# Folding every local product on GpSimd ahead of VectorE's sums, and output weights kept in dead key and query tiles

## The chip, the cores and the metric

The kernel runs on one core of a Trainium2 chip. A core has TensorE (matrix products, PE in the profile, with its weight loads as PEld), VectorE (DVE), ScalarE (ACT), GpSimd (POOL) and SyncE (SP), whose queue here issues nearly all DMAs. Each engine works through its own list of instructions in order and waits on the others through semaphores. The metric is the time of one execution on the device in microseconds, lower is better. Before the change the median of three runs is 921.38 us (920.93 to 921.93).

## The reference

Two attentions over the same x (2048 tokens, 448 columns, 16 heads of 28) are mixed by a gate of each token. Branch A looks at 8 keys per query, two tokens apart, backwards; branch B at all 2048 keys.

```python
def _A_ref(x, wqkv, wo):                       # W, dil = 8, 2
    q, k, v = qkv[0], qkv[1], qkv[2]
    idx = pos[:, None] - off[None, :]          # off = arange(W) * dil
    logits = jnp.einsum("bhsd,bhswd->bhsw", q, kg) * scale
    logits = jnp.where(mask[None, None, :, :], logits, -1e9)
    attn = _softmax(logits, axis=-1)
    o = jnp.einsum("bhsw,bhswd->bhsd", attn, vg)
    return o.transpose(0, 2, 1, 3).reshape(B, S, D) @ wo
def _B_ref(x, wqkv, wo):
    scores = jnp.einsum("bhqd,bhkd->bhqk", q, k) * (Dh ** -0.5)
    o = jnp.einsum("bhqk,bhkd->bhqd", _softmax(scores, axis=-1), v)
    return o.transpose(0, 2, 1, 3).reshape(B, S, D) @ wo
g = _sigmoid((x * gate_w).sum(-1, keepdims=True))
return g * a + (1 - g) * b
```

## The kernel before

All of it is float32 made from two halves: a value is split into a rounded part ("hi") and the rest ("lo"), and a product is three matmuls, hi·hi, hi·lo and lo·hi.

**Projection (to about 260 us).** q, k and v of both branches are formed and written to DRAM scratch (`qk_hi`, `qk_lo`, `a_scr`); v of branch B stays in the tile `V`.

**The 256 steps (about 260 to 843 us).** Branch B goes in 16 units u = 4·g + b, for head group g of four heads and query block b of 512. A unit has 16 steps, one for each block of 128 keys, so program step st = 16·u + kt. A step has, on TensorE, 12 score matmuls (four heads, three terms, L959) into pairs of PSUM banks, up to three matmuls of a first, rough pass over a later unit (L142, "maxima"), and the product of the step before with V (L925). ScalarE takes exp of two heads at a time (L962, two a step). VectorE takes the maximum of the rough scores from PSUM, one of 512 columns and one of 1024 a step (L146). The maxima of a unit are negated on GpSimd (`nmt`, L178), turned, stored and loaded back as two extra rows of the query tile `QH`, so that the exponent is already shifted. 320 of the 1024 rough tiles are done during the projection and three in each step after, so they end in step 234; the last 21 steps have scores, exp and V alone. This text calls these the bare steps. The key tiles `KH[1]`, `KH[2]`, `KL[0]` and the rough query tiles `QP[0]` have no reader in the last 40 steps.

**Branch A beside it.** Eight column groups c (two heads each) times eight offsets w. GpSimd multiplies q with the shifted k (`a_score`, L599, 128x896); for some (c, w) it also adds the upper 14 of each 28 columns onto the lower ("folds", L604, 128x448). VectorE sums along the row (`a_reduce`, L609): four pieces of 8 rows by 28 where the product is not folded, two of 16 rows by 14 where it is; each piece reads 224 elements. `NR[c, w]` holds the number of pieces: 2 for c < 2 and for odd w, else 4. Then come a softmax over w (`a_softmax`, shared by GpSimd, VectorE and ScalarE) and the weighted sum of v (`a_av`, L649 and L654, GpSimd alone), stored to `oa_scr`.

**What sets the order.** The steps are written out by hand; `at(place, st, f)` hangs a piece of work on a step ("pre" ahead of the scores, "dve" and "act" behind them, "end" last). Branch A is placed by a planner: `item` gives each piece an engine, a key (its wished step), an estimated cost and what it needs; `issue` emits pieces in the order of the keys while a running debt, `late`, stays under a limit (4.2 for GpSimd, `DLIM` for VectorE). The debt falls by `step` in each step and grows by the estimated cost, and for VectorE by a share for the rough maxima. The estimates order the work; they cost nothing themselves.

**The end.** When branch A is finished (`a_done`, program step 217 before), its memory is given back; the seven blocks of output weights `wo` are loaded (L742) and split by one ScalarE copy (L746) and one GpSimd subtraction (L747) each. After step 255 sixteen output tiles j follow (`op_tile`): the branch A rows are transposed (L781) and split, and 21 matmuls (L803) add both branches. `op_load_b(b, k)` brings piece k of branch B's normalised rows of query block b, `op_load_a(j)` those of branch A. A unit's result is finished in small pieces (`fin_*`): a copy of the V product on ScalarE (`osb`, L821), its sums through DRAM, a product and a subtraction on GpSimd (L850, L858) and a ScalarE copy (`onhi`, L854).

Of the kernel before, what the change touches and what calls it, by code (L numbers as in the profile page):

```python
# [25 lines left out]
def gated_mix_kernel(ctx: ExitStack, tc: tile.TileContext, xT, xn, gw, wA, wB, woAB, out):  # L26
# [568 lines left out]
    def a_score(c, w):  # L595
        if w == 0:
            Lt[c] = a2.tile([128, W, NJ, 2], F32, name="L", bufs=3)
        p = a3.tile([128, NJ, 56], F32, tag="prod", name="prod")
        nc.gpsimd.tensor_tensor(out=p, in0=qt[c], in1=kvt["k", c % 2][:, HALO - DIL * w:HALO - DIL * w + NJ, :],  # L599
                                op=ALU.mult)  # L600
        prods[c, w] = p.rearrange("p j (h d) -> p (j h) d", d=DH)
        if NR[c, w] == 2:
            lo, hi = prods[c, w][:, :, 0:DH // 2], prods[c, w][:, :, DH // 2:]
            nc.gpsimd.tensor_tensor(out=lo, in0=lo, in1=hi, op=ALU.add)  # L604
            prods[c, w] = lo
# [64 lines left out]
    for c in range(8):  # L670
        for w in range(W):
            NR[c, w] = 2 if w % 2 or c < 2 else 4
    last = lambda c, w: ("r", c, w, NR[c, w] - 1)
    for c in range(8):
        c0 = CH * c
# [4 lines left out]
        for w, o in enumerate((0, 2, 5, 8, 11, 14, 17, 20)):  # L680
            back = (c, w - 4) if w > 3 else (c - 1, w + 4)
            item("pool", c0 + o, ("s", c, w), 2.05 + 1.0 * (NR[c, w] == 2),
                 [(("ld", "k", c), 4), (("ld", "q", c), 4), (("a", c - 3, 7, 0), 0), (("s", c, w - 1), 0)]
                 + ([(last(*back), 0)] if back in NR else []), lambda c=c, w=w: a_score(c, w))
            for i in range(NR[c, w]):
                item("dve", c0 + o + 2 + 0.1 * i, ("r", c, w, i), 0.32,
                     [(("s", c, w), 3), (("r", c, w, i - 1) if i else last(c, w - 1) if w else ("r",), 0)],
                     lambda c=c, w=w, i=i: a_reduce(c, w, i, NR[c, w]))
# [7 lines left out]
        for w in range(W):  # L696
            for part in ((0,) if w == 0 else (0, 1)):
                item("pool", c0 + 30 + 1.4 * n, ("a", c, w, part), 1.65 if part == 0 else 2.05,
# [27 lines left out]
    A_START, DLIM, LOOK = 5, 0.7, 40  # L726
# [3 lines left out]
    wo = []  # L730
    wor = {}
    oP = {}

    def load_wo():
        actx.close()
        oP["1"] = ctx.enter_context(tc.tile_pool(name="wop", bufs=1))
        oP["2"] = ctx.enter_context(tc.tile_pool(name="wop2", bufs=2))
        wo.extend(oP["1"].tile([128, 7, D], F32R, name=f"wo{i}") for i in range(2))
# [5 lines left out]
    def split_wo(k):  # L744
        raw = wor.pop(k)[:, :D]
        nc.scalar.activation(wo[0][:, k, :], raw, AF.Copy)  # L746
        nc.gpsimd.tensor_tensor(out=wo[1][:, k, :], in0=raw, in1=wo[0][:, k, :].bitcast(F32), op=ALU.subtract)  # L747

    def a_done(st):
        adone.append(st)  # L750
        load_wo()

        d = -(st + 6) % NJ + 2 if (st + 6) % NJ > NJ - 7 else 0
        for k in range(7):
            at("pre", st + d + k + 1, lambda k=k: raw_wo(k))
            at("act", st + d + 6 + k, lambda k=k: split_wo(k))
# [41 lines left out]
    def op_mm(j, bank, ks, first=False, last=False):  # L798
        b, jj = divmod(j, 4)
        for k in ks:  # L800
            for i, (a, c) in enumerate(TERMS):
                src = oaT[j][a][:, 128 * k:128 * k + 128] if k < 3 else onT[b][k - 3][a][:, 128 * jj:128 * jj + 128]
                writes(bank, nc.tensor.matmul(bank[:, :D], src, wo[c][:, k, :],  # L803
# [92 lines left out]
    def op_tile(j, behind):  # L896
# [9 lines left out]
        if 4 <= j < 12:  # L906
            op_load_b(b + 1, j % 4)
# [58 lines left out]
    for u in range(NU):  # L966
        g, b = divmod(u, NB)
        for kt in range(NJ):
# [44 lines left out]
            step = 2.25 if left else 2.1  # L1013
            late["dve"] = max(0.0, late["dve"] + 0.58 * min(3, left) - step)
# [35 lines left out]
```

## Time and profile before

| what | before |
|---|---|
| median of 3 runs | 921.38 us |
| span of the profiled execution | 921.0 us |
| its own time, by the same start and end | 921.0 us, 0.38 us under the median |
| TensorE busy | 911.3 us (99%) |
| VectorE busy | 731.6 us (79%) |
| ScalarE busy | 649.8 us (71%) |
| GpSimd busy | 624.0 us (68%) |
| granted TensorE clock | 0.999 |

The shares are means over stages with different limits. Matmuls are pipelined, so a TensorE that is shown busy may still be late; whether a step could be shorter is read from the time between its exps, and what a step waits for from the waits. The order of instructions, shown below, tells where something stands in an engine's list, not when it runs.

### The profile page before, as it was taken

Reading aid. Unit: us, or ns where it says so; the run is one execution under the profiler, and the core shown is the slowest. Engines: PE = TensorE matmul, PEld = TensorE weight load, DVE = VectorE, ACT = ScalarE, POOL = GpSimd, SP = SyncE. Lnnn points to the kernel's source line nnn. Section 1 sums busy time; section 2 is a strip of 40 time slices with the busy share of each in tenths; the row PEclk is TensorE's granted clock in tenths of the full one; section 3 lists DMA queues with packets and bytes.
Section 4 is the critical chain, followed back from the end, with each engine's and each line's share of the span. In section 5 each row is a group of like instructions: output and inputs, shape, how many; then the busy total and the mean of one; then the engine's idle time right before and its main releaser. Section 6 shows DMA issues by size and latency. Waiting matters only on the chain.

```text
span 921.0 us, 21402 instructions
## 1 busy us (share of the span) xinstructions
PE 911.3 (99%) x8390; PEld 547.3 (59%) x8390; DVE 731.6 (79%) x975; ACT 649.8 (71%) x797; POOL 624.0 (68%) x488
## 2 busy tenths in 40 slices
PE   8999999999999999999999999999999999999998
PEld 6799999998944444444444444444444444335997
DVE  6488999998979999999999999999998888501221
ACT  6456434343378888888888888888989889996221
POOL 2389846464469799999999999999994851300100
PEclk9999999999999999999999999999999999999999
DMA  9877503559462342235135232431312123441572
GB/s 264 276 247 193 158 12 82 142 132 97 116 241 64 101 121 51 84 105 129 41 94 157 83 102 61 132 84 26 106 47 53 33 50 100 135 132 51 158 218 87
DMA packets 103966, 105.11 MB, mean 114 GB/s; under 512 B 64136, under 2 KB 73736, under 8 KB 103080
## 3 DMA queue, kind: packets, MB, share of 16 engines
q1 hardware_dynamic: 103720, 103.47, 41.5%
q8 instruction: 66, 1.08, 0.5%
q10 hardware_dynamic: 144, 0.26, 0.1%
q14 instruction: 36, 0.29, 0.1%
HBM read 62.72 MB, written 40.96 MB: 113 GB/s over the span
## 4 chain that ended last, share of the span: by engine, by line
PE 96%; DMA 2%; DVE 1%; ACT 1%; issue 0%; SPq 0%; ACTq 0%; DVEq 0%
PE T L959 31%; PE av L925 27%; PE r L295 15%; PE T L803 7%; PE r L290 6%; PE r L142 4%; PE T L142 4%; DMA V<-in_xT 1%; PE T L781 1%; DMA KH<-qk_hi 0%; DMA qk_hi<-qkh 0%; ACT P L962 0%; DVE xl L212 0%; SPq L99 0%; DVE MX L159 0%
## 5 line engine op out<-in xcount | busy, mean ns | idle before, releaser
L962 ACT ACTIVATE P<-T 128x1024 f32<-128x1024 f32 x512 | 497.0, 1024 | 66.0 <-PE T L959 64.9
L146 DVE TENSOR_REDUCE MX<-T 128x1 f32<-128x512 f32 x470 | 443.4, 954 | 39.2 <-PE T L959 16.4
L925 PE MATMUL av<-P,V 128*32 128x512 f32 x2048 | 272.7, 605 | 0.4 <-ACT osb L821 0.4
L959 PEld LDWEIGHTS T<-QH,KH 30*128 30x128 f32 x1024 | 92.5, 181 | 238.4 <-ACT P L962 197.5
L959 PE MATMUL T<-QH,KH 30*128 30x512 f32 x1024 | 222.9, 492 | 0.2 <-ACT P L962 0.2
L142 PE MATMUL T<-KH,QP 28*128 28x512 f32 x704 | 222.6, 463 | 0.1
L159 DVE TENSOR_REDUCE MX<-r 128x2 f32<-128x1024 f32 x160 | 192.1, 1222 | 27.1 <-PE r L142 23.4
L959 PE MATMUL T<-QH,KL 28*128 28x512 f32 x1024 | 190.8, 391 | 0.0
L959 PE MATMUL T<-QL,KH 28*128 28x512 f32 x1024 | 190.2, 392 | 0.0
L599 POOL TENSOR_TENSOR prod<-qt,kt 128x896 f32<-128x896 f32 x64 | 135.1, 2115 | 4.8 <-DMA kt<-a_scr 4.8
L358 ACT ACTIVATE raw<-r 128x896 f32<-128x896 f32 (+1 forms) x64 | 58.9, 921 | 99.4 <-PE r L295 93.7
L654 POOL TENSOR_TENSOR oat<-oat,prod 128x896 f32<-128x896 f32 x56 | 118.2, 2110 | 2.4
L142 PEld LDWEIGHTS T<-KH,QP 28*128 28x128 f32 x704 | 86.0, 181 | 23.2 <-ACT P L962 10.2
L359 POOL TENSOR_TENSOR ast<-raw 128x448 f32<-128x448 f32 x48 | 55.5, 1155 | 60.3 <-ACT raw L358 50.6
L649 POOL TENSOR_TENSOR prod<-vt,L 128x896 f32<-128x896 f32 x56 | 95.4, 1704 | 0.6
L959 PEld LDWEIGHTS T<-QH,KL 28*128 28x128 f32 x1024 | 93.5, 183 | 0.7
L959 PEld LDWEIGHTS T<-QL,KH 28*128 28x128 f32 x1024 | 93.4, 184 | 0.0
L925 PEld LDWEIGHTS av<-P,V 128*32 128x32 f32 x2048 | 40.3, 108 | 79.9 <-issue 66.8
L295 PE MATMUL r<-wh,xh 64*128 64x448 f32 (+1 forms) x512 | 82.8, 363 | 0.3 <-ACT raw L358 0.3
L142 PE MATMUL r<-KH,QP 64*128 64x512 f32 x320 | 80.5, 394 | 2.0 <-DMA KH<-qk_hi 0.8
L295 PE MATMUL r<-wh,xl 64*128 64x448 f32 (+1 forms) x384 | 70.4, 364 | 0.0
L295 PEld LDWEIGHTS r<-wh,xh 64*128 64x128 f32 x512 | 63.2, 185 | 1.5 <-ACT raw L358 0.6
(101 smaller groups left out, 1049.9 us busy)
## 6 DMA issues: line engine op xcount, KB each, us to landing
a_scr<-ast SPq DMA_DIRECT2D x24, 448.0 KB
qk_hi<-qkh SPq DMA_DIRECT2D x24, 256.0 KB
qk_lo<-qkh SPq DMA_DIRECT2D x24, 256.0 KB
rbc<-rs SPq DMA_DIRECT2D x64, 64.0 KB
QP<-qk_hi SPq DMA_DIRECT2D x64, 56.0 KB
KL<-qk_lo SPq DMA_DIRECT2D x16, 224.0 KB
QH<-qk_hi SPq DMA_DIRECT2D x64, 56.0 KB
QL<-qk_lo SPq DMA_DIRECT2D x64, 56.0 KB
```

Source lines behind the costliest of these rows:

```text
L142: nc.tensor.matmul(bank, qhis[u][h % 2][r, 128 * qs:128 * qs + 128], KH[u // NB % 3][r, 512 * kc:512 * kc + 512], start=True, stop=True)
L146: nc.vector.tensor_reduce(MX[:, n % NMX:n % NMX + k], bank, axis=X, op=ALU.max)
L159: nc.vector.tensor_reduce(m, PM[k], axis=X, op=ALU.max)
L295: nc.tensor.matmul(bank[:, 0:cols], x, ws[c][rows, k, 0:cols], start=first, stop=last)
L358: nc.scalar.activation(raw[:, :, 0:cols], PJ[n % 2][:, :, 0:cols], AF.Copy)
L599: nc.gpsimd.tensor_tensor(out=p, in0=qt[c], in1=kvt["k", c % 2][:, HALO - DIL * w:HALO - DIL * w + NJ, :], op=ALU.mult)
L649: nc.gpsimd.tensor_tensor(out=dst.rearrange("p j (h d) -> p j h d", d=DH), in0=kvt["v", c % 2][:, HALO - DIL * w:HALO - DIL * w + NJ, :].r ...
L654: nc.gpsimd.tensor_tensor(out=oat[c], in0=oat[c], in1=oat[c, w], op=ALU.add)
L803: writes(bank, nc.tensor.matmul(bank[:, :D], src, wo[c][:, k, :], start=(first and k == ks[0] and i == 0), stop=(last and k == ks[-1] and ...
L925: nc.tensor.matmul(av[32 * h:32 * h + 32, :], V[:, kt, 4 * g + h, :], tiles_[h], start=(kt == 0), stop=(kt == NJ - 1), skip_group_check=True)
L959: nc.tensor.matmul(bank[a], (KH[g % 3], KH[g % 3], KL[g % 2])[t][r, ks], (qh, ql, qh)[t][r, :], start=(t == 0), stop=(t == 2))
L962: nc.scalar.activation(p, one if a == "2" else mine, AF.Exp, scale=SCALE)
```

## The change

1. `NR` is 2 for all 64 products. GpSimd folds the 24 that it did not fold (c of 2 and above, even w), and VectorE sums each of these in two pieces instead of four. The planner's estimate for a product becomes 3.15, VectorE's limit `DLIM` goes from 0.7 to 0.6, its share for each rough tile from 0.58 to 0.6, and `step` from 2.25 to 2.2. The products and loads of c = 7 get keys five steps earlier.
2. The 14 pieces of the output weights have no tiles of their own. They lie in 448-column slices of `KH[1]`, `KH[2]`, `KL[0]` and the two tiles `QP[0]`. Their loads hang on steps 232 to 238 and their splits on steps 237 to 243, whenever branch A ends; before, both hung on the end of branch A, which put the splits on steps 226 to 232. The subtraction of the split moves from GpSimd to VectorE.
3. `a_done` falls on step 241. The first query block's rows (`op_load_b(0, k)`) are loaded four steps long after it, in place of steps 231 to 234; the second block's rows are loaded within output tiles 0 to 3, in place of steps 237 to 240. The first branch A rows are loaded at step 246, as before.

```diff
-        if NR[c, w] == 2:
-            lo, hi = prods[c, w][:, :, 0:DH // 2], prods[c, w][:, :, DH // 2:]
+        for n in (DH // 2, DH // 4)[:3 - NR[c, w]]:
+            lo, hi = prods[c, w][:, :, 0:n], prods[c, w][:, :, n:2 * n]
             nc.gpsimd.tensor_tensor(out=lo, in0=lo, in1=hi, op=ALU.add)
             prods[c, w] = lo
...
-            NR[c, w] = 2 if w % 2 or c < 2 else 4
+            NR[c, w] = 2
...
-        c0 = CH * c
+        c0 = CH * c - 5 * (c == 7)
...
-            item("pool", c0 + o, ("s", c, w), 2.05 + 1.0 * (NR[c, w] == 2),
+            item("pool", c0 + o, ("s", c, w), 3.15 + 0.5 * (NR[c, w] == 1),
...
-    A_START, DLIM, LOOK = 5, 0.7, 40
+    OP0 = NJ * (NU - 2)
+    WO_AT = OP0 + 8
+    A_START, DLIM, LOOK = 5, 0.6, 40
...
-    wo = []
+    spare = [t[:, D * i:D * i + D] for t in (KH[1], KH[2], KL[0]) for i in range(4)] + [t[:, :D] for t in QP[0]]
+    wo = [spare[:7], spare[7:]]
...
     def split_wo(k):
         raw = wor.pop(k)[:, :D]
-        nc.scalar.activation(wo[0][:, k, :], raw, AF.Copy)
-        nc.gpsimd.tensor_tensor(out=wo[1][:, k, :], in0=raw, in1=wo[0][:, k, :].bitcast(F32), op=ALU.subtract)
+        nc.scalar.activation(wo[0][k], raw, AF.Copy)
+        nc.vector.tensor_tensor(out=wo[1][k], in0=raw, in1=wo[0][k].bitcast(F32), op=ALU.subtract)
 
     def a_done(st):
         adone.append(st)
-        load_wo()
-
-        d = -(st + 6) % NJ + 2 if (st + 6) % NJ > NJ - 7 else 0
-        for k in range(7):
-            at("pre", st + d + k + 1, lambda k=k: raw_wo(k))
-            at("act", st + d + 6 + k, lambda k=k: split_wo(k))
+        assert st < OP0 + 24, st
+        actx.close()
+        oP["2"] = ctx.enter_context(tc.tile_pool(name="wop2", bufs=2))
+        for k in range(4):
+            at("end", st + 1 + k, lambda k=k: op_load_b(0, k))
+        at("end", st + 5, lambda: (op_load_a(0), op_load_a(1)))
+
+    for k in range(7):
+        at("pre", WO_AT + k, lambda k=k: raw_wo(k))
+        at("act", WO_AT + 5 + k, lambda k=k: split_wo(k))
...
-        if 4 <= j < 12:
+        if j < 12:
             op_load_b(b + 1, j % 4)
...
-    OP0 = NJ * (NU - 2)
-    for k in range(4):
-        at("end", OP0 + 7 + k, lambda k=k: op_load_b(0, k))
-        at("end", OP0 + 13 + k if k < 3 else OP0 + 16, lambda k=k: op_load_b(1, k))
-    at("end", OP0 + 22, lambda: (op_load_a(0), op_load_a(1)))
...
-            step = 2.25 if left else 2.1
-            late["dve"] = max(0.0, late["dve"] + 0.58 * min(3, left) - step)
+            step = 2.2 if left else 2.1
+            late["dve"] = max(0.0, late["dve"] + 0.6 * min(3, left) - step)
```

VectorE's list in the middle of the steps, before: `MX` rows are the two maxima of a step (128x1 and 128x2), `L<-prod` rows the sums of branch A; "x2" is two in a row.

```order
L609 TENSOR_REDUCE L<-prod 128x16 x2
L146 TENSOR_REDUCE MX<-T_3274 128x1
L146 TENSOR_REDUCE MX<-T_3266 128x2
L146 TENSOR_REDUCE MX<-T_3274 128x1
L146 TENSOR_REDUCE MX<-T_3262 128x2
L609 TENSOR_REDUCE L<-prod 128x8 x2
L146 TENSOR_REDUCE MX<-T_3274 128x1
L146 TENSOR_REDUCE MX<-T_3266 128x2
L609 TENSOR_REDUCE L<-prod 128x8
L146 TENSOR_REDUCE MX<-T_3274 128x1
```

The same list at about the same place, after:

```order
L609 TENSOR_REDUCE L<-prod 128x16
L146 TENSOR_REDUCE MX<-T_3274 128x1
L146 TENSOR_REDUCE MX<-T_3262 128x2
L609 TENSOR_REDUCE L<-prod 128x16
L146 TENSOR_REDUCE MX<-T_3274 128x1
L146 TENSOR_REDUCE MX<-T_3266 128x2
L609 TENSOR_REDUCE L<-prod 128x16
L146 TENSOR_REDUCE MX<-T_3274 128x1
L146 TENSOR_REDUCE MX<-T_3262 128x2
```

Where steps had none, one or two sums, each now has one at most; over the whole list 63 steps had two, and the sums reach to step 222 where they ended at step 199.

ScalarE's list, before, at the steps that held the weight copies (`wo_10159<-wor`), with three rough tiles in each step:

```order
L962 ACTIVATE P<-T_3270 128x1024
L962 ACTIVATE P<-T_3262 128x1024
L746 ACTIVATE wo_10159<-wor 128x448
L962 ACTIVATE P<-T_3270 128x1024
L962 ACTIVATE P<-T_3266 128x1024
L746 ACTIVATE wo_10159<-wor 128x448
```

After, the copies (now `KH<-wor`) stand between the exps of the bare steps 237 to 244, the fourth of them directly ahead of `osb`, the copy of unit 14's V product:

```order
L743 ACTIVATE KH_152<-wor 128x448
L958 ACTIVATE P<-T_3266 128x1024
L958 ACTIVATE P<-T_3262 128x1024
L743 ACTIVATE KH_152<-wor 128x448
L822 ACTIVATE osb<-av 128x512
L958 ACTIVATE P<-T_3270 128x1024
L958 ACTIVATE P<-T_3266 128x1024
L743 ACTIVATE KH_3279<-wor 128x448
```

The seven copies moved by eleven steps, out of steps with rough tiles into steps without.

GpSimd's list ahead of the last unit's maxima (`nmt`), after; before, `on` and seven weight subtractions stood there, and branch A had ended:

```order
L654 TENSOR_TENSOR oat<-oat,prod_10506 128x896
L649 TENSOR_TENSOR prod_10536<-vt_3306,L 128x896
L654 TENSOR_TENSOR oat<-oat,prod_10536 128x896
L851 TENSOR_TENSOR on<-osb,rbc 128x512
L178 TENSOR_TENSOR nmt<-nmv,nmt 128x16
L649 TENSOR_TENSOR prod_10628<-vt_3306,L 128x896
L654 TENSOR_TENSOR oat<-oat,prod_10628 128x896
```

The end of branch A now stands around `nmt` of unit 15, at program steps 228 to 236.

More of the change, by code (lines that the diff above doesn't have):

```diff
@@ L697, in gated_mix_kernel @@
             for part in ((0,) if w == 0 else (0, 1)):
-                item("pool", c0 + 30 + 1.4 * n, ("a", c, w, part), 1.65 if part == 0 else 2.05,
+                item("pool", CH * c + 30 + 1.4 * n, ("a", c, w, part), 1.65 if part == 0 else 2.05,
                      [(("m", c, 8), 0), (("ld", "v", c), 4),
@@ L725, in gated_mix_kernel @@
     adone = []
-    A_START, DLIM, LOOK = 5, 0.7, 40
-    wo = []
+    OP0 = NJ * (NU - 2)
[3 more added lines that the diff above has]
+    wo = [spare[:7], spare[7:]]
     wor = {}
     oP = {}
[L734 to L738, printed above, removed]
     def raw_wo(k):
@@ L802, in op_mm @@
                 src = oaT[j][a][:, 128 * k:128 * k + 128] if k < 3 else onT[b][k - 3][a][:, 128 * jj:128 * jj + 128]
-                writes(bank, nc.tensor.matmul(bank[:, :D], src, wo[c][:, k, :],
+                writes(bank, nc.tensor.matmul(bank[:, :D], src, wo[c][k],
                                               start=(first and k == ks[0] and i == 0),
```

## The prediction

> **What bounds the kernel now.** I read the page's busy shares first, then the chain that ended last, then the costliest groups and the waits, and last the windows around the steps that the change touches.
>
> ```profile
> PE 911.3 (99%) x8390; PEld 547.3 (59%) x8390; DVE 731.6 (79%) x975; ACT 649.8 (71%) x797; POOL 624.0 (68%) x488
> ...
> PE 96%; DMA 2%; DVE 1%; ACT 1%; issue 0%; SPq 0%; ACTq 0%; DVEq 0%
> ```
>
> TensorE is on 96% of the chain that ended last, VectorE and ScalarE on 1% each. The change adds and removes no matmul, so it can only move what TensorE waits for inside the steps. How long a step takes is seen by the exps, two to a step. The columns of the next view are: stretch, its length, ScalarE's busy time and number of exps, clock, DMA share, GB/s.
>
> ```profile
> 295.51:735.69 440.18, 372.69 (x384) 1.00 0.32 84
> 735.69:772.26 36.57, 31.05 (x32) 1.00 0.32 79
> 776.93:795.24 18.31, 15.73 (x16) 1.00 0.45 111
> 801.80:807.99 6.19, 5.82 (x7) 1.00 0.56 127
> 807.99:812.54 4.55, 3.90 (x4) 1.00 0.71 223
> 812.54:824.71 12.17, 11.60 (x12) 1.00 0.42 133
> 824.71:828.99 4.28, 3.88 (x4) 1.00 0.02 4
> 828.99:837.09 8.10, 7.73 (x8) 1.00 0.34 85
> ```
>
> The clock is full everywhere. The first row is steps 16 to 207, 192 steps of 2.2926 us; the second is unit 13, 16 steps of 2.2856 us. The third holds eight steps, seven of them with a weight copy: 2.289 us. Bare steps (sixth row) take 12.17 / 6 = 2.028 us.
>
> ```profile
> L962 ACT ACTIVATE P<-T 128x1024 f32<-128x1024 f32 x512 | 497.0, 1024 | 66.0 <-PE T L959 64.9
> L146 DVE TENSOR_REDUCE MX<-T 128x2 f32<-128x1024 f32 x234 | 286.3, 1223 | 20.2 <-PE T L959 11.5 <-PE T L142 0.2
> L146 DVE TENSOR_REDUCE MX<-T 128x1 f32<-128x512 f32 x236 | 162.0, 687 | 19.0 <-PE T L142 12.7 <-PE T L959 4.9
> L609 DVE TENSOR_REDUCE L<-prod x176: 327/375/382, 278.7 to 689.5; 128x8 f32<-128x224 f32 x96, 128x16 f32<-128x224 f32 x80
> ...
> L609 DVE TENSOR_REDUCE L<-prod 128x8 f32<-128x224 f32 x96 | 33.7, 371 | 0.0
> L609 DVE TENSOR_REDUCE L<-prod 128x16 f32<-128x224 f32 x80 | 28.3, 372 | 0.0
> ```
>
> The fourth row gives least, median and longest duration in ns, then the first and last start: branch A's sums end at 689.5 us. So unit 13 has VectorE work for the maxima alone, and its steps are only 2.2926 - 2.2856 = 0.007 us shorter. That is the size of what VectorE's load does to a step now.
>
> **The change part by part.**
>
> *Folds.* 24 more of this row's kind:
>
> ```profile
> L604 POOL TENSOR_TENSOR prod<-prod 128x448 f32<-128x448 f32 x40 | 41.0, 1026 | 3.1
> ```
>
> 24 x 1.026 = 24.6 us more on GpSimd. Its rows about the end of branch A:
>
> ```profile
> 747.06 2.11 POOL L654 TENSOR_TENSOR oat<-oat,prod 128x896 f32<-128x896 f32 x1
> 749.44 0.22 POOL L178 TENSOR_TENSOR nmt<-nmv,nmt 128x16 fp32r<-128x16 f32 x1 [0.28 <-ACT nmv L177]
> ...
> 799.89 3.86 ACT L962 ACTIVATE P<-T 128x1024 f32<-128x1024 f32 x4
> ```
>
> Branch A ended on GpSimd at 749.2 us; packed as tightly it would end at 773.8. The order puts its last addition at program step 236, whose exps start at 799.89. The result is first read by the transposes at step 254, whose ScalarE copy starts at 838.9:
>
> ```profile
> 838.93 0.50 ACT L789 ACTIVATE oah<-T 128x384 fp32r<-128x384 f32 x1
> ```
>
> What hides the 24.6 us is GpSimd's own free time between 749 and some 801 us; cost 0. If that cover were gone, the transposes would be late, up to the whole 24.6 us. [...]
>
> *Sums.* 24 products lose two pieces each: 48 x 0.372 = 17.9 us less on VectorE. In a step the two maxima take 0.687 + 1.223 = 1.91 us of 2.29; the 0.38 left holds one piece of 0.372, not two, and after the change no step has two. On the path this can give at most what unit 13 shows: 192 x 0.007 = 1.35 us. The other end is no gain, or a small loss, since the sums reach 23 steps further (23 x 0.007 = 0.16 us). The load falls by 48 of 216 pieces and all doubles go; I take two thirds, -0.9 us.
>
> *Weight copies.* Seven ScalarE copies leave steps with rough tiles, where eight steps took 18.31 us against 8 x 2.2856 = 18.28: they cost 0.03 us in all, because such a step leaves ScalarE idle. They enter bare steps, where ScalarE's rows read:
>
> ```profile
> 809.83 0.60 ACT L821 ACTIVATE osb<-av 128x512 f32<-128x512 f32 x1
> ...
> 812.55 3.86 ACT L962 ACTIVATE P<-T 128x1024 f32<-128x1024 f32 x4 [0.28 <-PE T L959]
> 816.60 3.88 ACT L962 ACTIVATE P<-T 128x1024 f32<-128x1024 f32 x4 [0.19 <-PE T L959]
> ...
> 824.71 3.88 ACT L962 ACTIVATE P<-T 128x1024 f32<-128x1024 f32 x4 [0.19 <-PE T L959]
> 828.47 0.63 ACT L854 ACTIVATE onhi<-on 128x512 fp32r<-128x512 f32 x1
> 828.99 3.87 ACT L962 ACTIVATE P<-T 128x1024 f32<-128x1024 f32 x4
> ```
>
> Four exps fill 3.87 of 4.06 us, so 0.19 us in two steps is all the room there is. The `onhi` copy at 828.47 is the nearest thing to an added copy: its two steps took 4.28 - 4.056 = 0.22 us more. The `osb` copy at 809.83 made its two steps 4.55 - 4.056 = 0.49 us longer, but it also holds up the V product that writes the bank it reads. Ends: 0 and 0.49 each; a weight copy holds no bank, so I take 0.22: 7 x 0.22 = 1.6 us. The copies queued behind: every later exp, and the V product behind each. The copy that stands directly ahead of `osb` has no idle room at all and may cost more.
>
> *Subtractions.* Seven, on VectorE instead of GpSimd. By the nearest row, seven of at most
>
> ```profile
> L340 DVE TENSOR_TENSOR qkh<-r,qkh 128x512 fp32r<-128x512 f32 x10 | 6.8, 688 | 7.5 <-ACT qkh L339 7.4
> ...
> 801.80:837.09 35.29, 34.85 (x346) 12.90 (x348) 0.25 (x1) 33.69 (x37) 2.80 (x3) 1.00 0.41 117
> 846.30:917.00 70.70, 70.70 (x373) 64.45 (x371) 15.00 (x36) 13.92 (x37) 2.80 (x3) 1.00 0.52 154
> ```
>
> 0.69 us each, 4.8 us in all. In the second row the busy times are TensorE, its loads, VectorE, ScalarE, GpSimd: VectorE has 0.25 us to do in those 35 us, so 0.
>
> *Loads.*
>
> ```profile
> 803.17 1.09 SPq L99 DMA_DIRECT2D QH<-nm  x2
> ...
> 823.44 1.29 POOL L850 TENSOR_TENSOR on<-osb,rbc 128x512 f32<-128x512 f32 x1 [5.01 <-DMA rbc<-rs]
> ```
>
> SyncE's list has four of the seven weight loads ahead of unit 15's query loads and three behind them, so these are issued near 804.3 and needed by the copies of steps 241 to 243, from 812 on. The first block's eight loads go behind branch A's last store and in among the small transfers of unit 14's result. That result's product ran on GpSimd at 823.44 to 824.73 and the `onhi` copy on ScalarE at 828.47, so 3.7 us are there before a late transfer holds up an exp; six loads ahead of it at some 0.45 us of SyncE each make 2.7. The second block's eight loads move into output tiles 0 to 3, behind stores that wait for each tile's result; the pieces of a block that are loaded in one group of four tiles and read in the next are what tiles 4 to 11 do already, and in the row of 846.30 TensorE was busy 70.70 of 70.70 us with them. So 0, with the other end one late load, which I bound by one tile's piece of SyncE's list, some 1 us. The keys of c = 7 only shift when its loads go out: 0.
>
> *Sum.* On the profiled execution's 921.0 us: -0.9 + 1.6 + 0 = +0.7, 921.7 us. The median is 0.38 us above this execution, so 922.1 us.
>
> **The rivals.** The bound used for "no change" is 0.2%, 1.84 us, about what a measurement of this kernel can tell.
>
> *A, slower: the copies cost what `osb` cost.* Place: bare steps 237 to 243. Each copy finds ScalarE full and V products waiting; price 7 x 0.49 = 3.4 us; with no gain from VectorE the time is 924.8. For: ScalarE's idle is 0.19 us in two steps, and one copy sits beside `osb`. Against: `onhi` cost less than half. It decides from (1.84 + 0.9) / 7 = 0.39 us per copy.
>
> *B, slower: GpSimd is late for the last maxima.* `nmt` of unit 15 now stands behind the end of branch A. Before, its chain was this:
>
> ```profile
> 797.47 0.22 POOL L178 TENSOR_TENSOR nmt<-nmv,nmt 128x16 fp32r<-128x16 f32 x1 [1.90 <-ACT nmv L177]
> ...
> 806.93 0.20 PEld L959 LDWEIGHTS T<-QH,KH 30*128 30x128 f32 x4 [0.84 <-issue]
> ```
>
> The last row is step 240, the first of unit 15: its extra rows are issued by 804.3 and read at 806.9, so at most 2.6 us is spare, less their time to land. If GpSimd is a whole product and addition late (1.7 + 2.1 = 3.8 us), TensorE waits 1 to 3.8 us: 923.1 to 925.9. For: GpSimd is packed there. Against: these products wait for no step of TensorE, so GpSimd can run ahead.
>
> *C, faster: VectorE is worth more than unit 13 shows.* The waits row, and under it the weight loads that waited for this line in two stretches (us, times), are
>
> ```profile
> PEld T L959 <- DVE MX L146: 9.1, 53, 0.5
> ...
> L146 DVE TENSOR_REDUCE MX<-T x350: 624/958/1228, 299.8 to 699.6; 128x1 f32<-128x512 f32 x175
>   PEld T L959: 5.8, 33
> ...
> L146 DVE TENSOR_REDUCE MX<-T x16: 692/958/1226, 758.8 to 776.4; 128x2 f32<-128x1024 f32 x8, 128x1 f32<-128x512 f32 x8
>   PEld T L959: 0.3, 2
> ```
>
> If its 9.1 us were all on the path and fell with the pieces (48 of 216), 2.0 us would go; with copies as cheap as before the time is 919.4. Against: the loads waited 5.8 us in the 400 us from 299.8 on and 0.3 us in the 17 from 760, where no sum of branch A is left: about 0.015 us per us in both.
>
> *D, the change does not do what it says:* VectorE's relief gives nothing. Then +1.6: 923.0, still within 0.2%.
>
> **How the numbers follow.** My sum and D, both within 0.2%: 0.50. A 0.21 and B 0.16 together are slower, 0.37. C and what lies beyond it, 0.13. The likeliest case is the sum, 922.1 us, with its own range from 920.1 (copies for nothing, all of 1.35 us gained) to 923.2. The range for 8 in 10 reaches to C and past A: 919.8 to 925.2 us.
>
> **What would show it.** Exps in steps 16 to 207 some 0.003 to 0.007 us closer per step if the sums are right. Steps 237 to 244 at about 2.25 us instead of 2.03 if the copies are right; 2.5 for A, and a wait of the first score matmuls of unit 15 on a DMA for B. GpSimd's last addition near 800 us and no wait of the transposes on it. VectorE's L609 at 128 pieces, some 45 to 48 us. Output tiles unchanged at about 4.7 us, 70.7 us in all. The forecast is wrong if a stretch outside steps 237 to 244 changes by over 1 us.

## The result, and the profile after

The changed kernel takes 922.27 us (median of 20 runs, 921.05 to 923.59) against 921.71 us for the kernel before (20 runs, 919.71 to 923.38): a ratio of 1.0008, 95% interval 1.0001 to 1.0015. By the bound of 0.2% nothing has changed; the interval puts the cost between 0.1 and 1.4 us.

The page's line of busy times and its line of the chain that ended last, after:

```profile
PE 912.2 (99%) x8390; PEld 546.5 (59%) x8390; DVE 728.8 (79%) x934; ACT 650.0 (71%) x797; POOL 640.6 (70%) x505
...
PE 95%; DMA 3%; SPq 1%; ACT 1%; POOL 0%; DVE 0%; issue 0%; ACTq 0%
```

GpSimd is busy 16.6 us longer (24.6 us of folds came, seven subtractions of 8.0 us in all went) and VectorE 2.8 us less. The span is 920.1 us, against 921.0 before, although the runs are slower. The reason lies ahead of the change: the first exp starts at 256.60 us after and at 258.73 before, with the same work ahead of it, and over all the profiles of this study it starts between 255.75 and 259.21 us. So spans are not compared here. What is compared is the time from one step's first exp to another's.

Exps by stretch, after: steps 16 to 207, unit 13 (208 to 223), 224 to 235, 236 to 244, 245 to 254. Columns are the stretch, its length, ScalarE's busy time with its exps, clock, DMA share, GB/s.

```profile
293.39:733.13 439.74, 372.87 (x385) 1.00 0.32 83
733.13:769.67 36.54, 31.08 (x33) 1.00 0.20 48
769.67:797.15 27.48, 23.31 (x25) 1.00 0.23 62
797.15:817.55 20.40, 17.80 (x18) 1.00 0.51 141
817.55:838.64 21.09, 19.35 (x21) 1.00 0.46 133
```

The last three of these stretches, before:

```profile
772.27:799.89 27.62, 23.49 (x25) 1.00 0.42 112
799.89:818.53 18.64, 17.43 (x18) 1.00 0.53 152
818.53:839.61 21.08, 19.35 (x22) 1.00 0.25 68
```

| steps | before | after | difference |
|---|---|---|---|
| 16 to 207 | 440.18 | 439.74 | -0.44 |
| 208 to 223 (unit 13) | 36.57 | 36.54 | -0.03 |
| 224 to 235 | 27.62 | 27.48 | -0.14 |
| 236 to 244 (the weight copies) | 18.64 | 20.40 | +1.76 |
| 245 to 254 | 21.08 | 21.09 | +0.01 |
| exp of step 255 to the end | 81.38 | 81.42 | +0.04 |

That adds up to +1.2 us, inside the interval of the ratio. One stretch carries it. ScalarE's rows there, after, show why (x2 is two exps in one row):

```profile
801.38 1.94 ACT L958 ACTIVATE P<-T 128x1024 f32<-128x1024 f32 x2
803.19 0.59 ACT L743 ACTIVATE KH<-wor 128x448 fp32r<-128x448 f32 x1
803.65 1.96 ACT L958 ACTIVATE P<-T 128x1024 f32<-128x1024 f32 x2
...
807.74 0.63 ACT L743 ACTIVATE KH<-wor 128x448 fp32r<-128x448 f32 x1
808.20 0.65 ACT L822 ACTIVATE osb<-av 128x512 f32<-128x512 f32 x1
808.68 2.01 ACT L958 ACTIVATE P<-T 128x1024 f32<-128x1024 f32 x2
```

No row of ScalarE in this stretch carries a wait, and ScalarE is busy in 20.40 of its 20.40 us: it is full. That it sets the pace here is tested below. The step from 801.38 to 803.65 lasts 2.27 us, where a bare step lasted 2.03: the two exps take 1.81 us from start to start (801.38 to 803.19) and the copy 0.46. So each copy first used up some 0.2 us that a bare step had to spare, and only the rest made the step longer. The step with a weight copy and `osb` lasts 2.75 (805.93, the exp ahead, to 808.68).

The smaller parts of the forecast, in the order sums, folds, VectorE's hold on the score weights:

```profile
L609 DVE TENSOR_REDUCE L<-prod x128: 326/376/379, 276.6 to 736.9; 128x16 f32<-128x224 f32 x128
L604 POOL TENSOR_TENSOR prod<-prod 128x448 f32<-128x448 f32 x64 | 65.6, 1026 | 5.0
PEld T L955 <- DVE MX L146: 8.4, 50, 0.5
```

128 sums instead of 176, the last one starting at 736.9 us; 64 folds of 1.026 us; and score weight loads that waited 8.4 us for the maxima instead of 9.1. GpSimd's rows around the end of branch A, after:

```profile
795.38 0.24 POOL L178 TENSOR_TENSOR nmt<-nmv,nmt 128x16 fp32r<-128x16 f32 x1
795.56 1.72 POOL L649 TENSOR_TENSOR prod<-vt,L 128x896 f32<-128x896 f32 x1
797.35 2.10 POOL L654 TENSOR_TENSOR oat<-oat,prod 128x896 f32<-128x896 f32 x1
...
824.59 1.28 POOL L851 TENSOR_TENSOR on<-osb,rbc 128x512 f32<-128x512 f32 x1 [7.73 <-DMA rbc<-rs]
```

Branch A ends on GpSimd at 799.45 us, and the first ScalarE copy of the transposed rows starts at 837.96, so the 24.6 us of folds are covered with 38 us between them. The output tiles are as before:

```profile
845.50:916.00 70.50, 70.48 (x372) 64.33 (x370) 14.99 (x36) 13.92 (x37) 2.80 (x3) 1.00 0.60 177
```

### The profile page after: what moved, and what is told of

Its sections match the earlier page's. It is cut to its first block, busy times and chain, and to the rows that moved or that the text cites. A ratio compares the mean times of both kernels' runs of the same rounds, so it can differ in the third digit from the quotient of the medians.

```text
span 920.1 us, 21384 instructions
## 1 busy us (share of the span) xinstructions
PE 912.2 (99%) x8390; PEld 546.5 (59%) x8390; DVE 728.8 (79%) x934; ACT 650.0 (71%) x797; POOL 640.6 (70%) x505
## 4 chain that ended last, share of the span: by engine, by line
PE 95%; DMA 3%; SPq 1%; ACT 1%; POOL 0%; DVE 0%; issue 0%; ACTq 0%
PE T L955 31%; PE av L921 28%; PE r L295 15%; PE T L804 7%; PE r L290 4%; PE r L142 4%; PE T L142 4%; DMA V<-in_xT 1%; DMA qk_hi<-qkh 1%; PE T L782 1%; DMA KH<-qk_hi 0%; SPq L217 0%; ACT P L958 0%; POOL wl L212 0%; DMA QP<-qk_hi 0%; ACT raw L358 0%
## 5 line engine op out<-in xcount | busy, mean ns | idle before, releaser
L146 DVE TENSOR_REDUCE MX<-T 128x1 f32<-128x512 f32 x470 | 448.9, 955 | 45.2 <-PE T L955 17.8
L142 PE MATMUL T<-KH,QP 28*128 28x512 f32 x704 | 225.0, 470 | 0.1
L604 POOL TENSOR_TENSOR prod<-prod 128x448 f32<-128x448 f32 x64 | 65.6, 1026 | 5.0
```

The source lines that it names most:

```text
L142: nc.tensor.matmul(bank, qhis[u][h % 2][r, 128 * qs:128 * qs + 128], KH[u // NB % 3][r, 512 * kc:512 * kc + 512], start=True, stop=True)
L146: nc.vector.tensor_reduce(MX[:, n % NMX:n % NMX + k], bank, axis=X, op=ALU.max)
```

## The experiments

In what follows "exp n" is the start of the first exp of step n. Each ratio is to the kernel before, on the same chip. Stretches are told against the changed kernel's or the kernel before's in the table above.

### The copies alone, in the kernel before

```diff
-            at("pre", st + d + k + 1, lambda k=k: raw_wo(k))
-            at("act", st + d + 6 + k, lambda k=k: split_wo(k))
+            at("pre", OP0 + 8 + k, lambda k=k: raw_wo(k))
+            at("act", OP0 + 13 + k, lambda k=k: split_wo(k))
```

> The kernel before with only the weight loads and splits moved to the changed kernel's steps (loads 232 to 238, splits 237 to 243, subtraction still on GpSimd, weights in their own tiles, products folded as before). Theory 1: steps 236 to 245 take 20.4 us instead of 18.64, the stretch from step 224 to 236 falls from 27.62 to about 27.5, the rest stays, and the whole is 1.7 us slower than the kernel before (ratio 1.0018). Rival: if the tiles or VectorE's subtraction matter, the stretch stays near 18.7.

```profile
797.97:818.36 20.39, 17.69 (x18) 1.00 0.61 187
```

922.9 us, ratio 1.0015 (1.0006 to 1.0023). The row is steps 236 to 244, 20.39 us, +1.75; steps 16 to 207 take 440.20, as before. The place of the copies makes the loss by itself, without the folds, the shared tiles or VectorE's subtractions: 0.25 us each.

### The copies taken off ScalarE, in the changed kernel

```diff
-        nc.scalar.activation(wo[0][k], raw, AF.Copy)
+        nc.vector.tensor_copy(wo[0][k], raw)
```

> The changed kernel with one line altered: the seven weight copies run on VectorE, which is idle in the bare steps, instead of ScalarE. Theory 1 (the copies' time on ScalarE is what the change costs): the stretch from the exps of step 236 to those of step 245 falls from 20.40 back to 18.6 us, to within 0.2, and the whole by 1.8 us, to about 0.998 of the changed kernel and 0.2 to 1.2 us under the kernel before. Rival (the loads, the VectorE subtractions or the key tiles that hold the weights are what makes these steps long): the stretch stays within 0.3 us of 20.40. A second rival, lateness of unit 15's extra query rows, which the copies now hide: the stretch falls by only about half, and the first weight load of unit 15 waits for a DMA.

```profile
797.22:815.97 18.75, 17.47 (x19) 1.00 0.49 131
815.97:837.29 21.32, 19.37 (x22) 1.00 0.52 151
```

920.63 us (919.94 to 921.34), ratio 0.9990 (0.9982 to 0.9999): ahead of both kernels, though the margin over the kernel before is 0.1%. The stretch with the copies is back at 18.75. What remains over the 18.6 forecast, and the 0.23 us that the next stretch gained, are two waits that the copies had covered:

```profile
804.35 0.41 PEld L955 LDWEIGHTS T<-QH,KH 30*128 30x128 f32 x4 [0.93 <-DMA QH<-nm]
```

That is the first score weight load of unit 15, which now waits for the extra rows (rival B). And on GpSimd and ScalarE:

```profile
824.82 1.28 POOL L851 TENSOR_TENSOR on<-osb,rbc 128x512 f32<-128x512 f32 x1 [9.15 <-DMA rbc<-rs]
```

```profile
826.13 0.63 ACT L855 ACTIVATE onhi<-on 128x512 fp32r<-128x512 f32 x1
```

`on` of unit 14 ends at 826.10 and `onhi` starts at 826.13: the copy that stands between exps waited for the product. In the changed kernel 1.6 us lay between the two (825.87 and 827.50), in the kernel before 3.7.

### Each copy twice

```diff
         nc.scalar.activation(wo[0][k], raw, AF.Copy)
+        nc.scalar.activation(wo[0][k], raw, AF.Copy)
```

> The changed kernel with every weight copy made twice in a row on ScalarE (14 copies). Theory 1 in its exact form (ScalarE is full in these steps, a copy takes 0.467 us from start to start): each second copy adds the whole 0.467 us, 7 x 0.467 = 3.3 us, so steps 236 to 245 take 23.7 us and the whole is 3.3 us over the changed kernel. Rival (a copy costs a fixed lost slot of about 0.25 us because it breaks the rhythm of exps and V products, not because ScalarE is full): the second copies add 0 to 1.8 us.

```profile
801.86 0.58 ACT L743 ACTIVATE KH<-wor 128x448 fp32r<-128x448 f32 x1
802.47 0.58 ACT L744 ACTIVATE KH<-wor 128x448 fp32r<-128x448 f32 x1
802.95 1.92 ACT L959 ACTIVATE P<-T 128x1024 f32<-128x1024 f32 x2
```

927.34 us, ratio 1.0060 (1.0043 to 1.0077). The stretch grew by 4.16 us over the changed kernel, 0.59 a copy, and not by 3.3. The rows give the difference: an exp starts 0.48 us after the copy ahead of it, before that copy has ended (802.47 + 0.58), but the second copy starts 0.61 us after the first, once it has ended. Both write the same tile. So the size of an added copy was 0.47 us only where its neighbours were exps; the direction, ScalarE as what bounds these steps, held.

### The folds alone undone

```diff
-            NR[c, w] = 2
+            NR[c, w] = 2 if w % 2 or c < 2 else 4
...
-        for n in (DH // 2, DH // 4)[:3 - NR[c, w]]:
+        for n in (DH // 2,) if NR[c, w] == 2 else ():
...
-            item("pool", c0 + o, ("s", c, w), 3.15 + 0.5 * (NR[c, w] == 1),
+            item("pool", c0 + o, ("s", c, w), 2.05 + 1.0 * (NR[c, w] == 2),
...
-    A_START, DLIM, LOOK = 5, 0.6, 40
+    A_START, DLIM, LOOK = 5, 0.7, 40
...
-        assert st < OP0 + 24, st
+        st = max(st, OP0 + 17)
```

The other numbers of the planner are those of the kernel before as well, and the loads stay where the change put them.

> The changed kernel with part 1 undone alone: 24 products are summed in four pieces again, the planner's numbers are those of the kernel before, weights and copies stay at the changed places, and the first output loads are held to step 242 and later. Theory 2 (VectorE's relief gives a little): steps 16 to 208 take 440.2 us as before instead of 439.74, and the whole is 0.3 to 1 us over the changed kernel. Rival (the 0.44 us between the two profiles is scatter of single late steps): the stretch lies anywhere in 439.6 to 440.6 and the medians of three-step groups are the same to 0.01 us.

```profile
293.96:734.19 440.23, 372.64 (x384) 1.00 0.32 84
```

922.89 us, ratio 1.0016 (1.0008 to 1.0025). Steps 16 to 207 return to 440.2 us and the copies still cost 1.75 (20.39 in their stretch). Part 1 of the change, folds and planner numbers together, is worth 0.45 to 0.5 us. This is not scatter between executions: steps 16 to 207 take 440.18 to 440.23 us in the three profiles with the old folds, and 439.62 to 439.87 in the nine with two pieces for every product. Where this comes from is seen by taking steps 6 to 203 in threes, since single steps vary by 0.1 to 0.2 us from one to the next. The median of three steps is 6.85 us in both kernels. What differs is how many of the 66 groups take over 6.95 us: nine before and nine here, beginning at the same steps (27, 57, 90, 93, 108, 126, 156, 165, 192), and five after (30, 93, 117, 126, 153). The other profiles agree: eight in the remaining one with the old folds, four to seven in the eight remaining with the new. The mean of a group is 6.879 us with the old folds and 6.871 with the new. Part 1 does not shorten the ordinary step; it removes a few late ones. Whether VectorE's shorter work does that or the other order of its list isn't separated by this run.

### One sum for the first three column groups

```diff
-            NR[c, w] = 2
+            NR[c, w] = 1 if c < 3 else 2
```

With this, 24 products are folded once more, to a quarter, and summed in one piece. Branch A ends later, and `a_done` falls on step 247.

> The changed kernel with NR = 1 for the first three column groups: 24 products are folded twice on GpSimd (a second fold of 128x224 each, about 0.5 us by half the 128x448 fold) and summed in one piece instead of two, so VectorE has 24 x 0.372 = 8.9 us less and GpSimd 12 us more, and branch A ends six steps later. Theory 2 (what VectorE's load costs are single late steps, 0.44 us between the two kernels): steps 16 to 208 take 439.2 to 439.8 us. Rival (each piece costs time by itself, as 48 pieces took 0.44): 439.5 from proportion alone, 439.74 - 0.22, which theory 2 doesn't exclude, so the count of late three-step groups over 6.95 us is looked at too: theory 2 has 3 to 5 of them. The end of branch A comes at step 247, so the first branch A rows are loaded at step 252, two steps ahead of the transposes: steps 245 to 255 or the first transposes may be late by 1 to 3 us, which says what the cover of GpSimd's longer work is worth.

```profile
814.71 2.37 POOL L654 TENSOR_TENSOR oat<-oat,prod 128x896 f32<-128x896 f32 x1
```

```profile
840.61 0.66 PE L782 MATMUL T<-ident,oal 128*128 128x128 f32 x4 [0.58 <-DMA oal<-oa_scr]
```

925.13 us, ratio 1.0037 (1.0023 to 1.0050). GpSimd's last addition starts at 814.71, counted from the first exp 16 us later than in the changed kernel, and now the transposes do wait for branch A's rows: step 254 takes 3.17 us, against 2.51. The first scores of unit 15 come late as well (step 239: 2.91). This is what the folds cost when their cover is gone. The other half missed: steps 16 to 207 took 440.37 us instead of the 439.2 to 439.8 expected. Only five groups are over 6.95 us and the median group is the shortest of all (6.848), but the five are later than the others' (1.85 us over 6.85 in all, against 0.97 in the changed kernel), and the mean group takes 6.881 us. Still less work on VectorE gained nothing here; which operation holds these steps isn't shown.

### The second block's loads moved back

```diff
         at("end", st + 5, lambda: (op_load_a(0), op_load_a(1)))
+        for k in range(4):
+            at("end", st + 6 + k, lambda k=k: op_load_b(1, k))
...
-        if j < 12:
+        if 4 <= j < 12:
```

> The changed kernel with the second block's eight output loads at steps 247 to 250 instead of output tiles 0 to 3. My forecast had 0 for this move: from step 255 to the end 81.4 us as in both kernels (81.38 and 81.42), to within 0.2, and the whole within 0.5 us of the changed kernel. Rival (the loads among the output tiles cost time): the end is shorter by 0.5 us or more.

921.82 us, ratio 1.0005 (0.9996 to 1.0015). From the exp of step 255 to the end it takes 81.18 us, against 81.42. Loading the second block inside output tiles 0 to 3 costs nothing that these runs can tell.

### The first block's loads later, with the copies on VectorE

```diff
-        nc.scalar.activation(wo[0][k], raw, AF.Copy)
+        nc.vector.tensor_copy(wo[0][k], raw)
...
-            at("end", st + 1 + k, lambda k=k: op_load_b(0, k))
+            at("end", st + 6 + k, lambda k=k: op_load_b(0, k))
```

> The changed kernel with the weight copies on VectorE and the first block's eight output loads five steps later (247 to 250), behind the broadcast of unit 14's result. In the kernel with these copies alone on VectorE, steps 245 to 255 took 21.32 us instead of 21.08, and the step of the onhi copy 2.58 instead of 2.35. Theory 3 (these loads, ahead of the broadcast in SyncE's list, make unit 14's product and so the onhi copy late by 0.25 us): the stretch falls to 21.08 and the broadcast is issued about 3 us earlier. Rival: lateness comes from the sums' way through DRAM or from GpSimd, and the stretch stays near 21.3.

```profile
816.40:837.50 21.10, 19.40 (x21) 1.00 0.58 168
```

920.75 us, ratio 0.9994 (0.9984 to 1.0003). The stretch from 245 is back at 21.10: `rbc` is issued 1.28 us after exp 245, against 5.23 us with the loads ahead of it, and `on` ends 3.85 us ahead of `onhi`. So it was these loads that held up unit 14's small transfers. The stretch before it got 0.25 us longer (19.00), by the wait at step 239 alone (2.48 us, against 2.23).

### Unit 14's copies on VectorE too

```diff
-        nc.scalar.activation(t, av, AF.Copy)
+        if u == NU - 2:
+            nc.vector.tensor_copy(t, av)
+        else:
+            nc.scalar.activation(t, av, AF.Copy)
...
-        nc.scalar.activation(fin["hi"], fin["on"], AF.Copy)
+        if u == NU - 2:
+            nc.vector.tensor_copy(fin["hi"], fin["on"])
+        else:
+            nc.scalar.activation(fin["hi"], fin["on"], AF.Copy)
```

The weight copies are on VectorE as well.

> The changed kernel with the weight copies on VectorE and also unit 14's two copies in the bare steps (osb and onhi) on VectorE. Theory 1: ScalarE then has exps alone until step 254; osb's 0.49 us and onhi's 0.22 to 0.47 go from steps 240 to 250 as well, so steps 236 to 245 take about 18.3 us, steps 245 to 255 20.8 us, and the whole is 0.6 to 0.9 us under the kernel with the weight copies alone on VectorE (920.63), near 919.9, under both kernels. Rival: VectorE's copies from PSUM are slower or wait, and the V product of step 241 still waits for osb: steps 236 to 245 stay at 18.75.

920.54 us, ratio 0.9989 (0.9980 to 0.9998), which can't be told from the weight copies on VectorE alone. Steps 245 to 254 came out as expected (20.86 us), steps 236 to 244 did not: 19.03 instead of 18.3. Step 241, behind `osb`, takes 1.93 us instead of 2.24 now that this copy is gone from ScalarE, but step 239 takes 2.64 us, since unit 15's extra rows come no earlier (their load goes out 0.3 us later).

### Unit 13's product behind the last maxima

Three kernels test whether GpSimd's list makes those rows late. All hang unit 13's normalising product, copy and subtraction four, two and one steps later:

```diff
-        l = {NU - 3: (1, 2, 5, 6, 9, 12, 13, 15), NU - 2: (1, 2, 5, 6, 8, 10, 10, 12)}.get(
+        l = {NU - 3: (1, 2, 5, 6, 13, 14, 14, 15), NU - 2: (1, 2, 5, 6, 8, 10, 10, 12)}.get(
```

The first has the weight copies on VectorE beside that, the second unit 14's two copies too, the third also the first block's loads at steps 247 to 250.

> The seven copies on VectorE, and beside that unit 13's normalising product moved on GpSimd from behind step 233 to behind step 237, so that the last maxima stand directly behind branch A's work. Theory (rival B's wait is real and comes from GpSimd's list): the step from exp 239 to 240, 2.23 us with the copies on VectorE alone, falls to 2.03 to 2.13 us, and steps 236 to 245 take 18.5 to 18.65 us (18.75 before that move). Rival (the wait comes from SyncE's queue or the transfer itself): the step stays at 2.2 us or more and the stretch at 18.75 or more. Total 920.4 in the one case, 920.6 in the other, which the time alone can't tell apart.

> The seven copies and unit 14's two copies on VectorE, and unit 13's normalising product behind step 237. Theory (the step of 2.64 us at 239 came from GpSimd's list ahead of the last maxima): that step falls to 2.2 us or less and steps 236 to 245 take 18.3 to 18.5 us (19.03 without the move); steps 245 to 255 stay at 20.9. Total 920.0. Rival (the delay comes from the transfers or from VectorE's copies, which run long beside GpSimd): the step stays at 2.4 us or more and the stretch at 18.8 or more; total 920.5.

> As the run before it, and the first block's rows loaded at steps 247 to 250 as well. If the small transfers of unit 14's result were delayed by those loads, steps 245 to 255 go from 20.9 to 20.3 to 20.8 us, with nothing else moved; if they only ate room, 20.9 stays. Total 919.8 to 920.1.

923.31 us, ratio 1.003 (1.0019 to 1.0041; expected 920.4 to 920.6); 920.91, 0.9993 (0.9984 to 1.0002); 920.9, 0.9996 (0.9984 to 1.0007). Step 239 took 2.54, 2.37 and 3.13 us, not 2.2 or less (the last in an execution 2.3 us slower than its kernel's median). The move did not do what it was made for. Two rows of the first of the three show it:

```profile
793.25 1.71 POOL L649 TENSOR_TENSOR prod<-vt,L 128x896 f32<-128x896 f32 x1
794.91 0.23 POOL L178 TENSOR_TENSOR nmt<-nmv,nmt 128x16 fp32r<-128x16 f32 x1
```

The planner filled the free place with a product of branch A, which is longer (1.71 us, against 1.29 for `on`), and `nmt` starts 3.30 us after exp 234, against 2.85 in the changed kernel and 2.23 before. So nothing here says what a shorter list would have given. The copy `onhi` of unit 13 moved with it, which gave steps 224 to 235 0.4 us (27.06) and took about 0.2 back in the next stretch.

The runs together do settle where the wait ends. The last column is the time from the issue of the load `QH<-nm` to exp 240, the first of unit 15. For the changed kernel it comes from these two rows:

```profile
801.83 1.05 SPq L99 DMA_DIRECT2D QH<-nm  x2
```

```profile
805.93 1.98 ACT L958 ACTIVATE P<-T 128x1024 f32<-128x1024 f32 x2
```

| kernel | `QH<-nm` issued after exp 234 | step 239 | issue to exp 240 |
|---|---|---|---|
| before | 7.93 | 2.13 | 4.83 |
| before, copies late | 9.88 | 2.30 | 3.56 |
| the change, folds undone | 7.93 | 2.27 | 5.50 |
| the change | 9.30 | 2.27 | 4.10 |
| the change, second block's loads moved back | 9.65 | 2.27 | 3.79 |
| each copy twice | 9.70 | 2.90 | 5.52 |
| copies on VectorE | 9.21 | 2.23 | 3.63 |
| the same, first loads later | 9.49 | 2.48 | 3.61 |
| unit 14's copies on VectorE too | 9.53 | 2.64 | 3.75 |
| unit 13's product later | 9.51 | 2.54 | 3.67 |
| all copies, product later | 9.49 | 2.37 | 3.55 |
| all copies, product and loads later | 10.09 | 3.13 | 3.71 |
| one sum for c < 3 | 10.43 | 2.91 | 3.60 |

In the last seven rows exp 240 comes 3.55 to 3.75 us after the issue, whatever the step before would have allowed. With the folds undone the load goes out as early as before the change, 1.4 us earlier than in it. 0.6 us of that is `nmt`, behind the longer list on GpSimd. The rest is SyncE's: it spent 2.40 us on the four loads just ahead, against 1.67 with the folds undone.

```profile
799.38 2.40 SPq L99 DMA_DIRECT2D QL<-qk_lo  x4
```

This second part doesn't need the folds. The kernel before with late copies has the old ones, and its `nmt` starts as early as before (2.23 us after exp 234); there these four took 2.56 us, weight loads stood among the loads ahead of them, and the extra rows went out 9.88 us after exp 234, so that this kernel too stands at the limit. What makes an issue on SyncE long isn't shown. The changed kernel itself is some 0.4 us away from that limit, and the kernel with the second block's loads moved back, with the same copies, less than 0.2, because the copies have made their steps longer.

The first of the three kernels lost 3.2 us more, in steps 245 to 254 (24.50 us, against 21.32 without the move); 1.5 us of that are the clock (last section). There SyncE issued two of the first block's loads ahead of `fsum`, `rbc` went out 6.95 us after exp 245, and `onhi` waited:

```profile
827.16 0.63 ACT L855 ACTIVATE onhi<-on 128x512 fp32r<-128x512 f32 x1 [1.77 <-POOL on L851]
```

With `onhi` off ScalarE the stretch is back at 20.9, and moving the first block's loads as well changes nothing more (20.88 and 20.87).

## Why the prediction was right

The forecast was 922.1 us and the median is 922.27. Its sum was +0.7 on the profiled execution; the stretches give +1.2. By its steps:

- **Weight copies, +1.6.** They cost 1.76 us in the changed kernel and 1.75 alone in the kernel before: 0.25 each, against the 0.22 taken from `onhi`. The room was larger than the forecast's "0.19 us in two steps": that was read from the ends of rows, but in the rows above an instruction starts about 0.1 us before the one ahead of it has ended (the copy at 803.19, the exps ahead of it to 803.32), so a step had some 0.2 us. Rival A (0.49 each) is out. The copy ahead of `osb` "may cost more" did not: steps 236 to 244 with `osb` are longer by 7 x 0.25 in all, and the step with both took 2.75 us, 0.47 more than its neighbours, where before `osb` made its two steps 0.49 longer.
- **Sums, -0.9.** Right in sign, twice too large: -0.44, and 0.45 to 0.5 by the run with the old folds. The step that was mis-sized is the gain of 1.35 us scaled by two thirds. It took the 0.007 us by which unit 13's steps are shorter as if each step shrank a little. The groups of three show that the ordinary step did not move; four late groups of nine went. The forecast of "0.003 to 0.007 us closer per step" came out at 0.44 / 192 = 0.0023. Three counts of the forecast and of the text ahead of it were off too: the sums before were 176, not 216, and in the trace 50 steps had two of them, not 63, and the last stood in step 188, not 199 (after: 210, not 222). Rival C would then be 2.5 us instead of 2.0; it is out either way: the weight loads' wait fell from 9.1 to 8.4 us.
- **Folds, 0.** Branch A ends at 799.45 us, as forecast from the order ("near 800"), and nothing waits for its rows. That the cover is finite is shown by the kernel with single sums, whose later end cost the transposes 0.66 us in step 254. That GpSimd takes 1.026 us for a fold that saves VectorE two sums of 0.372 costs nothing here for as long as GpSimd sets no end. Those are two different operations; the same operation on both engines is the weight subtraction, 1.14 us on GpSimd before and 0.63 on VectorE after.
- **Subtractions, 0.** The stretch of the copies is explained by ScalarE alone, since the kernel before with late copies has the subtractions on GpSimd and takes the same 20.39 us.
- **Loads, 0, with 1 us as the other end.** Right for this kernel: 21.09 and 81.42 us against 21.08 and 81.38. The forecast's "3.7 us are there" and 2.7 used were about the measure: 1.6 us stayed between `on` and `onhi`. But the bound of 1 us was too small for what lies past that room. With one more delay the same loads cost 3.2 us, 1.5 of it by the clock.
- **Rival B**, the late maxima, was the rival nearest to happening. Its mechanism is there in part (the extra rows go out 1.4 us later, 0.6 us of it by GpSimd and the rest by SyncE, which the forecast didn't consider), and its price in the changed kernel is nothing, since some 0.4 us are left. It was argued against by "GpSimd can run ahead", which is not what the runs show: GpSimd is packed and `nmt` does start 0.6 us later. What hides it is the loss by the copies, which the forecast had not connected with it. Taking the copies off ScalarE gave back 1.65 of the 1.76 us; the wait kept the rest, and took up to 1 us of step 239 in the other kernels (3.13 us, against 2.13 before).

That the total agrees to 0.2 us is partly luck. The two errors do not cancel: copies 0.16 us dearer and sums worth 0.46 less are together 0.6 us of cost more than forecast, and by the stretches the change costs 1.2 us, not 0.7. The medians differ by 0.56 us, and the interval, 0.1 to 1.4, holds all three figures. The kernel before was also 0.33 us slower in this comparison (921.71) than in the three runs that the forecast started from (921.38). The main mechanism, a ScalarE that is full in the bare steps, was right; the agreement of the number is finer than these runs can measure.

## What to carry to other kernels

Ask of each step which engine fills it: a copy of 0.6 us on ScalarE was free in steps with rough tiles (2.29 us, of which ScalarE's exps took 1.94 in unit 13) and cost 0.25 us in shorter ones that its exps already filled, and one line that gave it to an idle VectorE won it back. Work taken off an engine that isn't the bound removed late steps at a few places here, not time from every step, so count the late steps before pricing it. And a wait that costs nothing now may be hidden by the very loss you mean to remove: list the margins (here 0.4 us for unit 15's rows, 1.6 us for `on`) before counting the gain.

## What the runs showed of the hardware that was not expected

**TensorE's clock after a short idle.** In the kernel with unit 13's product later, TensorE idled 1.82 us at step 249:

```profile
828.75 0.50 PE L955 MATMUL T<-QH,KH 30*128 30x512 f32 x2 [1.82 <-ACT P L958]
...
829.67 1.94 PE L921 MATMUL av<-P,V 128*32 128x512 f32 x8
...
833.10 1.07 PE L921 MATMUL av<-P,V 128*32 128x512 f32 x8
```

Eight V matmuls took 1.94 us when they began 0.9 us after that idle time, and 1.07 us, as ever, when they began 4.3 us after it. The granted clock, window by window (after the length: TensorE, its loads, VectorE, ScalarE and GpSimd, then the clock):

```profile
829.00:830.00 1.00, 1.00 (x14) 0.44 (x14) 0.00 (x0) 1.00 (x2) 0.13 (x1) 0.81 0.61 141
830.00:831.00 1.00, 1.00 (x8) 0.00 (x0) 0.00 (x0) 1.00 (x2) 0.00 (x0) 0.50 0.62 139
832.00:833.00 1.00, 1.00 (x12) 0.37 (x8) 0.00 (x0) 0.00 (x0) 0.00 (x0) 0.50 0.57 163
833.00:833.50 0.50, 0.50 (x8) 0.16 (x8) 0.00 (x0) 0.23 (x1) 0.00 (x0) 0.97 0.91 338
```

It fell to one half from 829.6 to 833.0 us, 3.4 us, after TensorE was already at work again, and step 251 took 3.66 us instead of 2.12 (copies on VectorE alone). So of the 3.2 us lost in that stretch, 1.5 are the clock and not the wait. Not every execution shows a drop: five of the twelve had a mean clock of 0.998 (median 925.43 us), seven of 1.000 (922.75 us).

How much idle time it takes isn't shown, and no run was made to test it. TensorE's 0.58 us of waiting ahead of the transposes in step 254 of the kernel with single sums left the clock at 1.00 in each microsecond from 840 to 844 us. The profiled execution of the kernel with the second block's loads moved back has a mean clock of 0.998 too, though its steps 236 to 254 ran at 1.00.

**VectorE beside GpSimd.** With the weight copies on VectorE, the first of these copies and subtractions ran 2.5 to 4.6 times as long as later ones of the same shape. VectorE's rows, and GpSimd's of the same time:

```profile
795.87 1.74 DVE L743 CAST KH<-wor 128x448 fp32r<-128x448 f32 x1
797.64 2.41 DVE L744 TENSOR_TENSOR KH<-wor,KH 128x448 fp32r<-128x448 f32 x1
799.98 0.38 DVE L743 CAST KH<-wor 128x448 fp32r<-128x448 f32 x1
800.39 1.59 DVE L744 TENSOR_TENSOR KL<-wor,KH 128x448 fp32r<-128x448 f32 x1
802.32 0.63 DVE L744 TENSOR_TENSOR KL<-wor,KH 128x448 fp32r<-128x448 f32 x1
```

```profile
795.64 1.72 POOL L649 TENSOR_TENSOR prod<-vt,L 128x896 f32<-128x896 f32 x1
797.44 2.13 POOL L654 TENSOR_TENSOR oat<-oat,prod 128x896 f32<-128x896 f32 x1
800.18 1.31 POOL L859 TENSOR_TENSOR onlo<-on,onhi 128x512 fp32r<-128x512 f32 x1 [0.61 <-ACT P L958]
```

Each long VectorE row begins about 0.2 us after a GpSimd row and ends 0.25 to 0.5 us behind that row's end, as if it had run only then; those that begin with GpSimd idle take 0.38 and 0.63 us. The maxima and sums show none of it: in the kernel before, the longest maximum took 1.228 us between 299.8 and 699.6 us, with GpSimd busy in 384.9 of 399.8 us, and 1.226 us between 758.8 and 776.4, with GpSimd busy in 2.6 of 17.6 us; no sum took over 0.382 us. What makes the long rows long isn't shown: no run was made to separate GpSimd's work from another cause.
